# Second mixture: VectorE's two-SBUF-input operations moved in its order away from GpSimd's differences

## The chip, the cores and the metric

The kernel runs on 1 core of one Trainium2 chip. The metric is device time in microseconds (us), and the time of a version is the median of its runs. A profiled execution has a time of its own and a span, from its first instruction to its last.

## What is computed

Three layers in a row, in float32 (the weights come as float64), for 4 x 3072 tokens of 256 features:

```
scores = z @ z.T / 3072;  x = u * (max(scores, 0)**2 @ v)          # attention
k = max(mix(x, mu_k) @ w_k, 0);  x = sigmoid(mix(x, mu_r) @ w_r) * (k*k @ w_v)   # first mixture
out = ((x @ w_a) * (x @ w_b)) @ w_out                               # second mixture
```

The change lies in the second mixture alone: 12288 tokens, 256 features in and out, 1536 columns in `w_a` and `w_b`.

## The kernel before

**Precision.** Each float32 operand of a matmul is a pair: a high part rounded to float32r and a low part, the rest. ScalarE makes the high part with a copy (`high`, L1012), VectorE makes the low part with a subtraction of two SBUF tensors (`low`, L1015; L905 for the operands of the next pair). A product is three matmuls of 128x128 by 128x512: high by high, high by low, low by high.

**Units.** `mixture2` handles 12 pairs of blocks of 512 tokens (index j). For each pair it goes through 12 groups of columns (index f), so there are 144 units u = 12 j + f, and two more to drain. Each unit forms 2x2 block products with seven multiplications instead of eight (`PRODUCTS`, 1 to 7; L964), in three PSUM banks: `px`, `pw` and `py`, out of four. The order of a unit's matmuls is written out in `unit(u)`: product 1 of u; products 3 and 4 of the unit before (V = u - 1); products 2, 5 and 6 of u; two fillers; product 7 of u; the remaining fillers. A filler is one multiplication (three matmuls, L993 to L995) by `w_out` of work two units back or of the pair before. Units with f = 2 to 7 have three fillers, 30 matmuls in all; those with f = 8 to 11, and f = 0 and 1 of the next pair, have four, 33 matmuls.

**Around the matmuls.** Every engine works through its instructions in the order of the code, so the place of a line in `unit` is its place in its engine's queue. For V, VectorE adds product 3 (L1058, reads the bank `py`, which product 5 of u then takes), multiplies product 4 (L1073) and multiplies both (L1077, two SBUF inputs). If V is in the second half (f of V at least 6), L1087 forms both differences with the unit six earlier (`t32`), ScalarE rounds, and `low` gives `bl`; otherwise ScalarE rounds one block and `low` gives the low part of `b11`. L1141 adds product 7 of u to product 5 and frees `px` for product 4 in the next unit. GpSimd then forms one more difference from two SBUF tensors: L1149 for V in the second half, L1151 for V in the first.

**rest32.** For VV = u - 2 in the second half, `rest32` forms the low part `l32` of `t32` (128x1024, two SBUF inputs), used by the third and fourth filler of the same unit. It is called at f = 8 to 11 and f = 0 and 1 of the next pair, 6 units in 12. The high part `h32` is made by ScalarE a unit earlier.

**Hooks.** `run(slot)` calls what was hung on a unit's slots 0 to 10: loads of weights (`s_load` L935, `s4_load` L939, `o_load` L944 and L948, all on SP's queue, which takes them in order, each waiting for a free buffer of a pool of 25; weights asked for in unit k are first used in unit k + 2); the end of the pair before (`turn`, a transpose on VectorE, and `leave`, the stores); and the operands of the next pair, which need four differences t1 to t4 on GpSimd (`value`, L891) with high and low parts of these and of b11, b21 and b22.

Of the kernel before, what the change touches and what calls it, by code (L numbers as in the profile page):

```python
# [9 lines left out]
F32R = mybir.dt.float32r  # L10
# [17 lines left out]
def tile_kernel(  # L28
# [61 lines left out]
    def g_tile(shape, dtype, name):  # L90
        return gp.tile(shape, dtype, tag="g", name=name)
# [498 lines left out]
    def late_tile(shape, dtype, name):  # L590
        return late["p"].tile(shape, dtype, tag="m", name=name)

    def w_tile(dtype, name):
        return late["w"].tile([P, 2, QB], dtype, tag="w", name=name)
# [328 lines left out]
    def mixture2():  # L923
        NU = NP * NF2
        HALF = NF2 // 2
        back, forms, acc, ot, on, hooks = {}, {}, {}, {}, {}, {}
        sw, ow = {}, {}

        def hook(u, slot, *fns):
            hooks.setdefault((u, slot), []).extend(fns)  # L930
# [19 lines left out]
        def product(u, bank, n, first, end):  # L950
            j, f = divmod(u, NF2)
            a, b = PRODUCTS[n]
            t = t_t[j][b]
            r = u // 2
            if a == "s4":
                w = sw["D", r]
                c = f % TPB * P
                wh, wl = w[:, 0, c : c + P], w[:, 1, c : c + P]
            else:
                pair, k = PAIRS[a]  # L960
                c = f % 2 * P
                wh, wl = (sw[pair, r][:, k, h * (QB // 2) + c : h * (QB // 2) + c + P] for h in range(2))
            for m, (w, y) in enumerate(((wh, 0), (wh, 1), (wl, 0))):
                nc.tensor.matmul(  # L964
                    bank, w, t[:, y, :], start=first and m == 0, stop=end and m == 2, skip_group_check=True
                )
# [44 lines left out]
        def high(dst, src):  # L1011
            nc.scalar.activation(dst, src, AF.Copy)  # L1012

        def low(dst, src, hi):
            nc.vector.tensor_tensor(dst, src, hi.bitcast(F32), op=ALU.subtract)  # L1015

        def rest32(w, j, q):
            h, l, t = w["h32"], late_tile([P, 2, QB], F32R, "l32"), w["t32"]
            low(l, t, h)
            forms[j, q] |= {n: (h[:, k, :], l[:, k, :]) for k, n in enumerate(("t2", "t3"))}  # L1020

        def unit(u):
            j, f = divmod(u, NF2)
            go = u < NU
            v, vv = u - 1, u - 2
            V = back[v] if 0 <= v < NU else None
            VV = back[vv] if 0 <= vv < NU else None
            vj, vf = divmod(v, NF2)
            wj, wf = divmod(vv, NF2)
            vq, wq = vf % HALF, wf % HALF  # L1030
            v2, w2 = vf >= HALF, wf >= HALF
            todo = fillers(u) if go else []

            def run(slot):
                for fn in hooks.pop((u, slot), ()):
                    fn()
# [9 lines left out]
            if go:  # L1046
                x, w = U["x"], U["w"] = ps_tile("px"), ps_tile("pw")
                product(u, x, 1, True, False)
                nc.scalar.activation(w, x, AF.Copy)  # L1049
            if VV and w2 and vv < NU - 1:  # L1050
                rest32(VV, wj, wq)
            run(0)

            if V:
                cc = V["cc"]
# [6 lines left out]
            if VV and not w2:  # L1062
                t1 = w_tile(F32R, "th")
# [17 lines left out]
            if VV and w2:  # L1081
                h = g_tile([P, 2, QB], F32R, "t4")
                high(h[:, 0, :], VV["cc"][:, 0, :])
                VV["h4"] = h
            if V and v2:
                t = V["t32"] = back[v - HALF]["cc"]
                nc.vector.tensor_tensor(  # L1087
                    t, cc[:, 1, :].unsqueeze(1).to_broadcast([P, 2, QB]), t, op=ALU.subtract
                )
# [23 lines left out]
            if VV and w2:  # L1113
                h = VV["h4"]
                low(h[:, 1, :], VV["cc"][:, 0, :], h[:, 0, :])
                forms[wj, wq]["t4"] = (h[:, 0, :], h[:, 1, :])
            if V:
                if not go:
                    rest32(V, vj, vq)
                if v2:  # L1120
                    h, l = w_tile(F32R, "bh"), w_tile(F32R, "bl")
                    high(h, cc)
                    low(l, cc, h)
                    forms[vj, vq] |= {n: (h[:, k, :], l[:, k, :]) for k, n in enumerate(("b21", "b22"))}
                else:
                    h = w_tile(F32R, "b11")
                    high(h[:, 0, :], cc[:, 0, :])
                    low(h[:, 1, :], cc[:, 0, :], h[:, 0, :])
                    forms[vj, vq] = {"b11": (h[:, 0, :], h[:, 1, :])}
            run(5)  # L1130

            fill()
# [2 lines left out]
            fill()  # L1135
            run(7)

            if go:
                product(u, x, 7, False, False)
                cu = U["cc"] = g_tile([P, 2, QB], F32, "cc")  # L1140
                nc.vector.tensor_tensor(cu[:, 1, :], x, m5, op=ALU.add)  # L1141
# [28 lines left out]
        def turn(j, n, d):  # L1170
            if (j, n) not in on:
                on[j, n] = stp.tile([P, QB // SQ, ND, SQ], F32, tag="st", name="on")
            o = on[j, n]
            nc.vector.transpose(o[:, :, d, :], ot[j, n][:, d, :].rearrange("p (b i) -> p b i", i=SQ))

        def leave(j, n, queues=None):
            queues = queues or [nc.sync] * 4
            o = on.pop((j, n))
            r = out[(2 * j + n) * QB : (2 * j + n + 1) * QB, :]
            for a, dst in enumerate(r.rearrange("(b i) (a h j) -> a i b (h j)", i=SQ, h=ND, j=SQ)):  # L1180
                queues[a].dma_start(dst, o[a * SQ : (a + 1) * SQ].rearrange("i b h j -> i b (h j)"))
# [4 lines left out]
        def middle(j):  # L1186
            acs = acc[j]
            acs["B"] = accp.tile([P, QB], F32, tag="acc", name="oacc")
            nc.scalar.activation(acs["B"], acs["A"], AF.Copy)
# [17 lines left out]
        def c12_out(j):  # L1207
            scaled(ot[j, 1][:, 0, :], acc[j].pop("D"))
# [17 lines left out]
        for j in range(NP):  # L1226
            u = j * NF2
            hook(u + 7, 8, lambda j=j: middle(j))
            hook(u + 7, 9, lambda j=j: middle2(j))
            if j < NP - 1:  # L1230
                e = u + NF2
                hook(e + 1, 8, lambda j=j: c11_out(j))
                hook(e + 1, 10, lambda j=j: a_copy(j))
                hook(e + 2, 0, lambda j=j: add_to(j, "D"))
                hook(e + 2, 1, lambda j=j: add_to(j, "G"))
                hook(e + 2, 2, lambda j=j: c12_out(j))
                hook(e + 2, 3, lambda j=j: c22_sum(j))
                hook(e + 2, 8, lambda j=j: c22_out(j))
                hook(e + 3, 6, lambda j=j: turn(j, 1, 0))
                hook(e + 3, 9, lambda j=j: turn(j, 1, 1), lambda j=j: leave(j, 1))  # L1240
                hook(e + 4, 9, lambda j=j: turn(j, 0, 0))
                hook(e + 7, 10, lambda j=j: c21_out(j))
                hook(e + 8, 8, lambda j=j: turn(j, 0, 1), lambda j=j: leave(j, 0))
            if j:
                value, hi, lo = prep(j)
                todo = [
                    (1, 8, hi["b11"]), (2, 3, value["t1"]), (2, 9, lo["b11"]),
                    (3, 3, value["t2"]), (3, 7, hi["t1"]), (3, 8, lo["t1"]), (3, 8, hi["b21"]),
                    (4, 3, value["t4"]), (4, 4, lo["b21"]), (4, 7, hi["t2"]), (4, 8, lo["t2"]),
                    (5, 3, value["t3"]), (5, 6, hi["t4"]), (5, 7, lo["t4"]), (5, 8, hi["t3"]),  # L1250
                    (6, 4, lo["t3"]), (6, 8, hi["b22"]), (7, 4, lo["b22"]),
                ]
                for f, slot, fn in todo:
                    hook(u - NF2 + f, slot, fn)
                hook(u - NF2, 3, lambda j=j: y_load(j))
            for r in range(HALF):
                R = j * HALF + r
                k = 2 * R - 2
                if R > 1:
                    hook(k, 0, lambda R=R: s_load(R, "A"), lambda R=R: s_load(R, "B"))  # L1260
                    hook(k, 1, lambda R=R: s_load(R, "C"))
                    if R % 2 == 0:
                        hook(k - 1 if R > 2 else k, 3, lambda R=R: s4_load(R))
                loads = {
                    0: [(j - 1, 2, 2), (j - 1, 3, 2)],
                    1: [(j - 1, 4, 0), (j, 1, 0)],
                    2: [(j, 1, 1)],
                    3: [(j - 1, 4, 1), (j, 1, 2)],
                    4: [(j, 2, 0), (j, 3, 0)],
                    5: [(j, 2, 1), (j, 3, 1)],  # L1270
                }[r]
                for l in loads:
                    if l[0] >= 0:
                        hook(max(k, 0), 7, lambda l=l: o_load(*l))
        j = NP - 1
# [100 lines left out]
    with tc.manual_schedule():  # L1376
# [9 lines left out]
        turn, high, low = z_prep(0, 0)  # L1386
# [55 lines left out]
```

## Time and profile before

| what | value |
|---|---|
| median of 3 runs | 2589.59 us (2589.27 to 2591.72) |
| profiled execution, its own time | 2590.21 us |
| its span | 2588.4 us |
| TensorE busy with matmuls (PE) | 2554.8 us, 11112 matmuls |
| VectorE (DVE) busy | 2124.8 us |
| ScalarE (ACT) busy | 1847.3 us |
| GpSimd (POOL) busy | 326.2 us |
| second mixture without its drain, in the span | 1515.3 to 2566.7 us |

Busy time is the union of an engine's instructions. Matmuls overlap in the records, so TensorE counts as busy even where it gets on more slowly than it could; the number of matmuls in a stretch tells its pace. PEld is the loading of a matmul's 128x128 weights, which goes on beside the matmul before it.

### The profile page before, as it was taken

To read this page: it belongs to the slowest core of one execution; us is meant where nothing else is said; L and a number is where in the kernel's file an instruction comes from. 1 tells how busy PE (TensorE), PEld (TensorE's weight loads), DVE (VectorE), ACT (ScalarE), POOL (GpSimd) and SP (SyncE) were. 2 spreads that over 40 slices of the span, in tenths; PEclk is the share of its full clock that TensorE was granted. 3 is DMA by queue.
4 is the path that set the end of the run, shared out by engine and by line. 5 is a ranking of instruction groups with operands and counts; after the bars stand their busy time and mean duration, and the time that the engine had idled before them with its cause. 6 is when DMAs were issued, how large, how long until landed. Compare 5 with 4: busy or idle time off the path is not lost.

```text
span 2588.4 us, 32030 instructions
## 1 busy us (share of the span) xinstructions
PE 2554.8 (99%) x11112; PEld 2082.7 (80%) x11112; DVE 2124.8 (82%) x2785; ACT 1847.3 (71%) x2538; POOL 326.2 (13%) x320
## 2 busy tenths in 40 slices
PE   8999999999999999999999999999999999999998
PEld 6887888788788887888888877788788778877886
DVE  9887888788778778778787769888888988898888
ACT  7866977787588658878888766666666666666655
POOL 0010100010001100000000012222122222222211
PEclk9999999999999999999999999999999999999999
DMA  8788779767967793121121255665766575657563
GB/s 211 216 232 199 247 204 248 203 220 230 216 184 215 219 256 103 49 96 51 58 90 49 78 191 187 205 218 175 252 207 208 180 255 193 222 196 239 188 200 121
DMA packets 326017, 473.18 MB, mean 183 GB/s; under 512 B 192544, under 2 KB 205856, under 8 KB 318176
## 3 DMA queue, kind: packets, MB, share of 16 engines
q1 hardware_dynamic: 304832, 372.31, 49.6%
q0 software_dynamic: 18384, 98.31, 9.9%
q8 instruction: 87, 1.43, 0.2%
q10 hardware_dynamic: 2640, 0.52, 0.1%
q14 instruction: 74, 0.61, 0.1%
HBM read 347.60 MB, written 123.47 MB: 182 GB/s over the span
## 4 chain that ended last, share of the span: by engine, by line
PE 91%; DVE 3%; ACT 2%; DMA 2%; issue 1%; SPq 0%; DVEq 0%; ACTq 0%
PE px L964 14%; PE acc L101 9%; PE acc L102 9%; PE acc L100 9%; PE py L964 8%; PE px L682 5%; PE oacc L995 4%; PE oacc L993 4%; PE oacc L994 4%; PE pw L964 3%; PE vacc L100 3%; PE vacc L101 3%; PE vacc L102 3%; PE sc L440 3%; PE sc L441 3%; PE py L682 2%
## 5 line engine op out<-in xcount | busy, mean ns | idle before, releaser
L101 PE MATMUL acc<-lo,vhi 128*128 128x512 f32 x1152 | 451.3, 392 | 3.9 <-DVE lo L502 3.9
L100 PE MATMUL acc<-hi,vhi 128*128 128x512 f32 x1152 | 450.3, 391 | 3.1 <-ACT hi L499 1.9
L102 PE MATMUL acc<-hi,vlo 128*128 128x512 f32 x1152 | 450.1, 391 | 0.0
L964 PE MATMUL px<-t,sw 128*128 128x512 f32 x1296 | 365.1, 390 | 0.1
L964 PEld LDWEIGHTS px<-t,sw 128*128 128x128 f32 x1296 | 243.2, 188 | 52.6 <-DVE cc L1141 0.7
L101 PEld LDWEIGHTS acc<-lo,vhi 128*128 128x128 f32 x1152 | 217.1, 188 | 51.9 <-DVE lo L502 7.0
L100 PEld LDWEIGHTS acc<-hi,vhi 128*128 128x128 f32 x1152 | 217.2, 189 | 50.1 <-ACT hi L499 3.3
L453 ACT ACTIVATE p<-sc 128x1024 f32<-128x1024 f32 x167 | 170.6, 1021 | 116.9 <-PE sc L441 115.5
L102 PEld LDWEIGHTS acc<-hi,vlo 128*128 128x128 f32 x1152 | 217.3, 189 | 44.7
L1049 ACT ACTIVATE pw<-px 128x512 f32<-128x512 f32 x144 | 84.1, 584 | 201.7 <-PE px L964 201.7
L460 DVE STREAM_TRANSPOSE pt<-p 128x512 f32<-128x512 f32 x240 | 156.2, 689 | 74.6 <-ACT p L454 71.5
L1151 POOL TENSOR_TENSOR cc<-cc 128x512 f32<-128x512 f32 x72 | 96.8, 1344 | 881.4 <-DVE b L1015 674.0
L502 DVE TENSOR_TENSOR lo<-p,hi 128x1024 fp32r<-128x1024 f32 x167 | 199.7, 1196 | 4.9
L454 ACT ACTIVATE p<-p 128x1024 f32<-128x1024 f32 x167 | 177.2, 1061 | 5.3
L502 DVE TENSOR_TENSOR lo<-pm,hi 128x1024 fp32r<-128x1024 f32 x120 | 146.0, 1217 | 34.0 <-ACT hi L499 34.0
L1099 ACT ACTIVATE c<-pw 128x512 f32<-128x512 f32 x144 | 86.3, 599 | 117.7 <-PE pw L964 98.8
L101 PE MATMUL vacc<-kl,w 128*128 128x512 f32 x384 | 149.7, 390 | 0.6 <-DVE kl L753 0.6
L1149 POOL TENSOR_TENSOR cc<-cc 128x512 f32<-128x512 f32 x71 | 91.6, 1290 | 459.4 <-DVE bl L1015 285.2
L102 PE MATMUL vacc<-kh,w 128*128 128x512 f32 x384 | 149.5, 389 | 0.0
L100 PE MATMUL vacc<-kh,w 128*128 128x512 f32 x384 | 149.5, 389 | 0.0
L440 PE MATMUL sc<-q,kt 128*128 128x512 f32 x336 | 133.1, 396 | 6.6 <-DVE q L373 6.5
L1015 DVE TENSOR_TENSOR l<-cc,h 128x1024 fp32r<-128x1024 f32 x72 | 138.6, 1926 | 0.5 <-ACT h L1012 0.5
(194 smaller groups left out, 6018.8 us busy)
## 6 DMA issues: line engine op xcount, KB each, us to landing
sw<-kept SPq DMA_DIRECT2D x252, 512.0 KB, 5.9
pkept<-pt POOLq DMA_DIRECT2D x60, 1024.0 KB, 6.0
pm<-pkept SPq DMA_DIRECT2D x240, 256.0 KB, 6.4
ow<-kept SPq DMA_DIRECT2D x120, 512.0 KB, 7.1
kept<-w POOLq DMA_DIRECT2D x42, 512.0 KB, 5.6
vst<-in_v SPq DMA_DIRECT2D x24, 512.0 KB, 7.6
ust<-in_u SPq DMA_DIRECT2D x192, 64.0 KB, 4.6
xkept<-x POOLq DMA_DIRECT2D x24, 512.0 KB, 4.1
```

The lines of the kernel that those rows point to most:

```text
L100: nc.tensor.matmul(ps, wh, ah, start=first, stop=False)
L101: nc.tensor.matmul(ps, wh, al, start=False, stop=False)
L102: nc.tensor.matmul(ps, wl, ah, start=False, stop=last)
L440: nc.tensor.matmul(sc[:, t, :], k, q_t[b, qb][:, 0, :], start=True, stop=False)
L453: nc.scalar.activation(p, sc, AF.Relu, scale=1.0 / S)
L454: nc.scalar.activation(p, p, AF.Square)
L460: nc.vector.transpose(pt[:, :, 2 * pr + t, :], p[:, t, :].rearrange("p (c i) -> p c i", i=SQ))
L502: nc.vector.tensor_tensor(l, p, h.bitcast(F32), op=ALU.subtract)
L682: nc.tensor.matmul(bank, w[x][:, c], t[:, y, :], start=first and m == 0, stop=end and m == 2, skip_group_check=True)
L964: nc.tensor.matmul(bank, w, t[:, y, :], start=first and m == 0, stop=end and m == 2, skip_group_check=True)
L993: nc.tensor.matmul(acs[bank], wh, hi, start=first, stop=False, skip_group_check=True)
L1015: nc.vector.tensor_tensor(dst, src, hi.bitcast(F32), op=ALU.subtract)
```

## The change

`rest32` moves from the start of a unit, ahead of L1058, to behind L1077. The low part of `b11` moves from its place behind the high part to just ahead of product 7, behind slot 7. In the hooks, the transposes move from slots 6 and 9 to slots 4 and 8, the four differences of the next pair move to slot 9, right behind GpSimd's own difference of the unit, and all low parts of the next pair to slot 4; the high parts are at slot 8. Several of these come up to a unit earlier. No instruction is added or removed.

```diff
-            if VV and w2 and vv < NU - 1:
-                rest32(VV, wj, wq)
             run(0)
...
                 VV["h4"] = h
+                if vv < NU - 1:
+                    rest32(VV, wj, wq)
             if V and v2:
                 t = V["t32"] = back[v - HALF]["cc"]
...
-                    h = w_tile(F32R, "b11")
-                    high(h[:, 0, :], cc[:, 0, :])
-                    low(h[:, 1, :], cc[:, 0, :], h[:, 0, :])
-                    forms[vj, vq] = {"b11": (h[:, 0, :], h[:, 1, :])}
+                    b11 = w_tile(F32R, "b11")
+                    high(b11[:, 0, :], cc[:, 0, :])
             run(5)
...
             run(7)
 
+            if V and not v2:
+                low(b11[:, 1, :], cc[:, 0, :], b11[:, 0, :])
+                forms[vj, vq] = {"b11": (b11[:, 0, :], b11[:, 1, :])}
             if go:
                 product(u, x, 7, False, False)
...
-                hook(e + 3, 6, lambda j=j: turn(j, 1, 0))
-                hook(e + 3, 9, lambda j=j: turn(j, 1, 1), lambda j=j: leave(j, 1))
-                hook(e + 4, 9, lambda j=j: turn(j, 0, 0))
+                hook(e + 3, 4, lambda j=j: turn(j, 1, 0))
+                hook(e + 3, 8, lambda j=j: turn(j, 1, 1), lambda j=j: leave(j, 1))
+                hook(e + 4, 8, lambda j=j: turn(j, 0, 0))
...
-                    (1, 8, hi["b11"]), (2, 3, value["t1"]), (2, 9, lo["b11"]),
-                    (3, 3, value["t2"]), (3, 7, hi["t1"]), (3, 8, lo["t1"]), (3, 8, hi["b21"]),
-                    (4, 3, value["t4"]), (4, 4, lo["b21"]), (4, 7, hi["t2"]), (4, 8, lo["t2"]),
-                    (5, 3, value["t3"]), (5, 6, hi["t4"]), (5, 7, lo["t4"]), (5, 8, hi["t3"]),
-                    (6, 4, lo["t3"]), (6, 8, hi["b22"]), (7, 4, lo["b22"]),
+                    (1, 8, hi["b11"]), (1, 9, value["t1"]), (2, 4, lo["b11"]),
+                    (2, 8, hi["t1"]), (2, 9, value["t2"]), (3, 4, lo["t1"]), (3, 8, hi["b21"]),
+                    (3, 8, hi["t2"]), (3, 9, value["t4"]), (4, 4, lo["b21"]), (4, 4, lo["t2"]), (4, 8, hi["t4"]),
+                    (4, 9, value["t3"]), (5, 4, lo["t4"]), (5, 8, hi["t3"]),
+                    (5, 8, hi["b22"]), (6, 4, lo["t3"]), (6, 4, lo["b22"]),
```

## Rows read from the trace of the kernel before

**Rows 1.** The page, part 1: busy time of each engine, share of the span, instructions.

```profile
PE 2554.8 (99%) x11112; PEld 2082.7 (80%) x11112; DVE 2124.8 (82%) x2785; ACT 1847.3 (71%) x2538; POOL 326.2 (13%) x320
```

**Rows 2.** Busy time by stretch: f = 2 to 7, then f = 8 to 1.

```profile
core 0: us, PE busy (x) PEld busy (x) DVE busy (x) ACT busy (x) POOL busy (x), PEclk, DMA share, GB/s
2142.66:2183.50 40.84, 40.84 (x181) 33.78 (x180) 32.99 (x50) 26.95 (x47) 12.00 (x10) 1.00 0.59 198
2183.50:2230.72 47.22, 46.68 (x199) 36.63 (x198) 43.51 (x50) 29.64 (x46) 9.39 (x8) 1.00 0.67 220
```

**Rows 3.** Waits of weight loads, second mixture: us in total, times, longest us.

```profile
PEld py L964 <- DVE u L1058: 35.7, 75, 1.2
...
PEld px L964 <- DVE cc L1141: 0.7, 2, 0.6
```

**Rows 4.** Groups by line and shape, second mixture: busy us, mean ns | idle before, releaser.

```profile
L1015 DVE TENSOR_TENSOR l<-cc,h 128x1024 fp32r<-128x1024 f32 x70 | 135.4, 1934 | 0.0
L964 PE MATMUL py<-t,sw 128*128 128x512 f32 x432 | 130.5, 410 | 7.5 <-DVE u L1058 6.3 <-ACT c L1099 0.7
L964 PE MATMUL pw<-b,sw 128*128 128x512 f32 x432 | 122.8, 393 | 0.5 <-ACT pw L1049 0.5
...
L964 PE MATMUL py<-b,sw 128*128 128x512 f32 x429 | 120.5, 389 | 0.0
...
L1015 DVE TENSOR_TENSOR bl<-cc,bh 128x1024 fp32r<-128x1024 f32 x71 | 87.0, 1225 | 19.9 <-ACT bh L1012 19.4
```

**Rows 5.** Timeline of a unit with f = 11: start us, us, instruction.

```profile
1941.52 0.68 DVE L1141 TENSOR_TENSOR cc<-px,m 128x512 f32<-128x512 f32 x1
...
1941.82 1.29 POOL L1149 TENSOR_TENSOR cc<-cc 128x512 f32<-128x512 f32 x1 [6.50 <-DVE bl L1015]
1941.95 0.84 PE L964 MATMUL px<-b,sw 128*128 128x512 f32 x3
1942.12 2.08 DVE L1015 TENSOR_TENSOR l<-cc,h 128x1024 fp32r<-128x1024 f32 x1
...
1944.12 0.68 DVE L1058 TENSOR_TENSOR u<-py,u 128x512 f32<-128x512 f32 x1
...
1944.85 0.96 PE L964 MATMUL py<-t,sw 128*128 128x512 f32 x3
...
1945.32 0.68 DVE L1077 TENSOR_TENSOR cc<-u,cc 128x512 f32<-128x512 f32 x1
...
1945.65 0.85 PE L964 MATMUL px<-t,sw 128*128 128x512 f32 x3
...
1946.03 1.23 DVE L1087 TENSOR_TENSOR cc<-cc 128x1024 f32<-128x1024 f32 x1
...
1947.08 1.05 ACT L1012 ACTIVATE bh<-cc 128x1024 fp32r<-128x1024 f32 x1
1947.17 0.69 DVE L1015 TENSOR_TENSOR t<-cc,t 128x512 fp32r<-128x512 f32 x1
...
1948.17 1.22 DVE L1015 TENSOR_TENSOR bl<-cc,bh 128x1024 fp32r<-128x1024 f32 x1 [0.31 <-ACT bh L1012]
...
1949.61 1.29 POOL L1149 TENSOR_TENSOR cc<-cc 128x512 f32<-128x512 f32 x1 [6.50 <-issue]
```

**Rows 6.** Timeline of the end of f = 6 and of f = 7, without rest32.

```profile
1909.94 0.69 DVE L1015 TENSOR_TENSOR b<-cc,b 128x512 fp32r<-128x512 f32 x1 [0.69 <-ACT b L1012]
...
1911.31 0.84 PE L964 MATMUL px<-b,sw 128*128 128x512 f32 x3
...
1912.87 0.69 DVE L1058 TENSOR_TENSOR u<-py,u 128x512 f32<-128x512 f32 x1 [1.35 <-PE py L964]
...
1914.03 0.84 PE L964 MATMUL py<-t,sw 128*128 128x512 f32 x3
...
1914.16 0.68 DVE L1077 TENSOR_TENSOR cc<-u,cc 128x512 f32<-128x512 f32 x1
```

**Rows 7.** Second mixture: SP's wait for rest32's buffers; landing of the loads of sw.

```profile
SPq L935 <- DVE l L1015: 118.6, 23, 7.0
...
DMA to landing us min/median/max: 3.3/5.9/11.1
```

## Prediction

> **What bounds the kernel now.** I read the page first: the reader is to see TensorE at 99% of the span and VectorE at 82%, so time can only come from places where TensorE, although it counts as busy, gets on too slowly [rows 1]. The change touches only the second mixture, so I cut one pair of blocks of that stage into its two halves and asked for the busy time of each. The six units f = 2 to 7 take 40.84 us for 180 matmuls, 0.2269 us each, with VectorE busy for 33.0 us. The six units f = 8 to 11 and f = 0, 1 of the next pair take 47.22 us for 198 matmuls, 0.2385 us each, with VectorE busy for 43.5 us [rows 2]. At the pace of the first half, 198 matmuls take 198 x 0.2269 = 44.92 us, so each second half loses 47.22 - 44.92 = 2.30 us. I call its units full units: they are the ones with four fillers, and the ones that call rest32.
>
> The waits say where. In all of the second mixture TensorE's weight loads wait 75 times on `u L1058`, 35.7 us in total, and on nothing else in VectorE but 0.7 us for `cc L1141` [rows 3]. By lines, the matmuls of product 5 (`py<-t,sw`) last 410 ns in the mean, where the same shape lasts 389 ns in product 3, and have 7.5 us of idle time ahead of them [rows 4].
>
> The timeline of one full unit shows why [rows 5]. Count from the first matmul of product 1, at 1941.95. L1141 runs, GpSimd's difference L1149 starts at 1941.82, and the low part `l<-cc,h` of rest32 starts at 1942.12. It takes 2.08 us; the low part of the same shape `bl<-cc,bh` takes 1.23 us in the same unit and 1225 ns in the mean of 71, against 1934 ns for the 70 of rest32 [rows 4, 5]. L1058 can only follow, at 1944.12. It frees the bank that product 5 writes, and product 5 starts at 1944.85, 2.90 us after product 1. In a unit without rest32, L1058 starts 1.56 us after product 1 and product 5 starts 2.72 us after it [rows 6].
>
> VectorE's own order in this unit has no room: its instructions follow each other from L1141 at 1941.52 to `bl` at 1948.17 and then L1141 again [rows 5], 7.8 us in all against 33 x 0.2269 = 7.49 us of matmuls. So the full units run at VectorE's pace, and 0.85 us of it is rest32 beside GpSimd.
>
> On that overlap the page "SBUF — State Buffer" of the Trainium skill, section "Who interferes with whom", says that a VectorE instruction with two SBUF inputs and a GpSimd instruction that reads SBUF exclude each other for the whole instruction, whichever starts first. The trace agrees here: GpSimd ends at 1943.11, and 1.09 us later, at 1944.20, rest32's low part is done, about what such an instruction takes if it begins at GpSimd's end. If instead any VectorE work beside GpSimd lost 0.85 us, the sum below would stay as it is, because VectorE has 0.90 us idle where GpSimd will run.
>
> **The change part by part.** *rest32 goes behind L1077.* It issues one VectorE instruction and no DMA. I lay out a full unit from rows, product 1 at 0. L1058 starts at 1.56 and L1077 at 2.85 [rows 6]. An instruction of 512 columns holds VectorE for 0.60 us (L1058 to L1077 is two of them in 1.20 us), one of 1024 columns alone for 1.14 us (L1087 at 1946.03 to `t` at 1947.17) [rows 5]. So rest32 runs from 3.45, L1087 from 4.59, the low part of t4 from 5.73, `bl` from 6.33. For `bl` ScalarE's `bh` must be done: it starts 1.43 us after product 6 does and `bl` 1.09 us after that [rows 5]; product 6 starts after 15 matmuls, at 3.40, so `bl` could start at 5.92, and it is VectorE's order that sets 6.33. L1141 follows at 7.47 and ends at 8.15. The next unit begins at 7.49.
>
> What is late next, and by how much it is not. Product 5 needs L1058's end at 2.24 and starts at 2.72: 0.48 us to spare. The third filler needs rest32's result at its third matmul, the thirtieth of the unit: 29 x 0.2269 = 6.58, and it is there at 3.45 + 1.23 = 4.68. Product 4 of the next unit adds to the bank that L1141 reads: it starts at 7.49 + 1.36 = 8.85, and L1141 is done at 8.15, 0.70 us to spare, the tightest place. GpSimd's difference starts 1.44 us after `bl` [rows 5], at 7.77, and ends at 9.06, beside L1141 (one input in PSUM; it took 0.68 us beside GpSimd at 1941.52 [rows 5]) and an idle VectorE (8.15 to 9.05, when the next L1058 is due). The next L1077, with two SBUF inputs, comes at 7.49 + 2.85 = 10.34, 1.28 us after. So nothing waits for VectorE any more and the unit takes 7.49 us.
>
> Sum: 70 of these low parts lie ahead of the drain, 70 / 6 = 11.7 halves x 2.30 = 26.8 us. What stays is product 2's wait on ScalarE's L1049, which the change doesn't touch: the 432 matmuls of `pw` last 393 ns instead of 389, 1.7 us [rows 4]. Gain 26.8 - 1.7 = 25.1 us. Bounds: TensorE's own rows alone give 432 x 21 ns + 7.5 us = 16.6 us for product 5 [rows 4]; more than 26.8 us would need time outside the full units.
>
> *The SP queue that rest32 is moved past.* rest32 is the last reader of a `cc` buffer, and loads of `sw` wait for it: SP waited 23 times on it, 118.6 us [rows 7]. Its end goes from 2.25 us after product 1 to 4.68, so such a load is issued up to 2.4 us later, with those behind it. Loads asked for in unit k are first used in unit k + 2, about 15 us on, and land 5.9 us after issue in the median, 11.1 us at most [rows 7]. No row of the waits has TensorE waiting for a load. I cost it at nothing; without that cover it is the rival on the other side.
>
> *Low part of b11 behind the fillers, the transposes and low parts of the next pair at slots 4 and 8, differences at slot 9.* All of it lies in units with f = 1 to 6, where VectorE is busy for 33.0 of 40.8 us and TensorE keeps its pace [rows 2]. Two differences in a row hold GpSimd for about 2 x 1.29 us [rows 5] after the low part of b11 `b<-cc,b`, which ends 0.7 us before the next unit [rows 6]; with about 0.2 us for GpSimd to start they end 2.0 us into it, ahead of L1077 at 2.85. Nothing gained, and nothing lost as long as L1058 ends before 2.72. Low parts freed from GpSimd there save VectorE time that nobody waits for: zero. ScalarE's high parts move with them and are no more in number. *The drain:* the same L1058, L1077, rest32 and L1087 in another order before the chain that ends the kernel; L1087 comes at about the same time. Zero, within about 1 us either way.
>
> **The rivals.** *The wait moves to product 4 (12%).* L1141 now ends a long run of VectorE. If one of the four long instructions still meets GpSimd and takes 0.85 us more, L1141 ends 0.85 - 0.70 = 0.15 us late in each full unit: 70 x 0.15 = 10.5 us come back, gain 14.6 us, 2575 us. For it: the margin is the smallest one. Against it: now product 4 waits on L1141 twice in all [rows 3], and GpSimd is released by `bl`, the last of the run.
>
> *No change (5%).* L1058 would have been held not by rest32 but by product 3, or GpSimd's difference would slide along to the new place. Then 2589 to 2591 us. Against it: L1058 starts 2.17 us after product 1, 0.61 us later than in a unit without rest32 [rows 5, 6], and just as rest32 ends.
>
> *Slower by the loads (4%).* If `sw` loads released by rest32 landed just when TensorE needs them, each of the 23 waits would pass on 2.4 us: 55 us lost against 25 gained, about 2619 us. The place is product 1 of the unit after next; it breaks even where the loads have 25.1 / 23 = 1.1 us less to spare than the 2.4 us. Against it: some 15 us of lead against a landing of 5.9 us.
>
> **How the numbers follow.** The forecast as told, 79%. The profiled execution took 2590.21 us, 0.62 us over the median of the runs, and the gain of 25.1 us comes off it: 2565.1 us in that execution, 2564.5 us as a median. The range begins at 2560, where the wait for ScalarE and a little of the other units go too, and ends at 2574, where only the 16.6 us of TensorE's own rows come back; it leaves out the rivals and a little of the forecast, 2 in 10. A kernel whose runs lie within 0.1% of each other tells 0.2%, 5 us, from no change. Faster by more than that: 0.91 (the forecast and the first rival); within it 0.05; slower 0.04.
>
> **What would show it.** In the profile after: rest32's low part at about 1.23 us and behind L1077; the 75 waits on `u L1058` gone from the full units; product 5 at 2.72 us after product 1; full halves of about 45.1 us, other halves unchanged at 40.8. Wrong, if weight loads wait on `cc L1141` or on `sw`, if GpSimd's L1149 grows or starts beside L1077, or if the halves with f = 2 to 7 get longer.

## The result, and the profile after

The changed kernel takes 2561.49 us (median of 5 runs, 2559.63 to 2564.64) against 2589.49 us before (5 runs, 2588.93 to 2591.72): 28.0 us less, ratio 0.9892, 95% interval 0.9878 to 0.9907. The forecast was 2564.5 us. The profiled execution took 2563.22 us (span 2561.5 us), against 2590.21 us: 27.0 us less. In the changed kernel some lines have other numbers: L1058 is L1056, L1073 is L1071, L1077 is L1075, L1141 is L1142 and L1149 is L1150.

The two halves of the same pair of blocks as in [rows 2], f = 2 to 7 and then f = 8 to 1:

```profile
2126.33:2167.13 40.80, 40.80 (x181) 33.81 (x180) 32.23 (x49) 26.96 (x47) 11.13 (x10) 1.00 0.64 216
2167.13:2212.19 45.06, 45.06 (x199) 37.12 (x198) 39.37 (x50) 30.18 (x46) 9.38 (x8) 1.00 0.68 223
```

The first half is as it was. The second, the one with the full units, went from 47.22 to 45.06 us: 0.2276 us for a matmul instead of 0.2385. VectorE is busy there for 39.4 us instead of 43.5 with as many instructions.

All that the weight loads of the second mixture still wait for, up to the end of the drain (answers to [rows 3]: us in total, times, longest us):

```profile
PEld pw L964 <- ACT pw L1049: 3.9, 12, 0.9
PEld oacc L995 <- DVE l L1015: 1.1, 1, 1.1
PEld py L964 <- ACT c L1099: 1.1, 1, 1.1
PEld px L964 <- DVE cc L1142: 0.9, 2, 0.6
PEld oh L995 <- DVE t L1015: 0.7, 1, 0.7
```

The 75 waits on `u L1058`, 35.7 us, are gone altogether; the 12 on ScalarE's L1049 are what they were, and no load of weights is waited for. By lines (answers to [rows 4]):

```profile
L964 PE MATMUL pw<-b,sw 128*128 128x512 f32 x432 | 122.9, 393 | 0.5 <-ACT pw L1049 0.5
L964 PE MATMUL py<-t,sw 128*128 128x512 f32 x432 | 121.6, 390 | 0.7 <-ACT c L1099 0.7
...
L1015 DVE TENSOR_TENSOR bl<-cc,bh 128x1024 fp32r<-128x1024 f32 x71 | 86.6, 1220 | 7.7 <-ACT bh L1012 7.7
...
L1015 DVE TENSOR_TENSOR l<-cc,h 128x1024 fp32r<-128x1024 f32 x70 | 85.3, 1219 | 0.0
```

rest32's low part now lasts 1219 ns, as long as `bl` of the same shape, and the matmuls of product 5 (`py<-t`) 390 ns, next to the 389 ns of product 3 in [rows 4]. The timeline of a full unit (answers to [rows 5]: start us, us, instruction):

```profile
1930.19 1.22 DVE L1015 TENSOR_TENSOR bl<-cc,bh 128x1024 fp32r<-128x1024 f32 x1
...
1931.33 0.69 DVE L1142 TENSOR_TENSOR cc<-px,m 128x512 f32<-128x512 f32 x1
1931.35 0.84 PE L964 MATMUL px<-b,sw 128*128 128x512 f32 x3
1931.56 1.29 POOL L1150 TENSOR_TENSOR cc<-cc 128x512 f32<-128x512 f32 x1 [6.19 <-DVE bl L1015]
...
1932.91 0.69 DVE L1056 TENSOR_TENSOR u<-py,u 128x512 f32<-128x512 f32 x1 [0.90 <-PE py L964]
...
1934.07 0.84 PE L964 MATMUL py<-t,sw 128*128 128x512 f32 x3
1934.20 0.68 DVE L1075 TENSOR_TENSOR cc<-u,cc 128x512 f32<-128x512 f32 x1
...
1934.80 1.22 DVE L1015 TENSOR_TENSOR l<-cc,h 128x1024 fp32r<-128x1024 f32 x1
...
1935.94 1.22 DVE L1087 TENSOR_TENSOR cc<-cc 128x1024 f32<-128x1024 f32 x1
...
1937.07 0.69 DVE L1015 TENSOR_TENSOR t<-cc,t 128x512 fp32r<-128x512 f32 x1
...
1937.67 1.22 DVE L1015 TENSOR_TENSOR bl<-cc,bh 128x1024 fp32r<-128x1024 f32 x1
1938.81 0.69 DVE L1142 TENSOR_TENSOR cc<-px,m 128x512 f32<-128x512 f32 x1
1938.83 0.84 PE L964 MATMUL px<-b,sw 128*128 128x512 f32 x3
```

GpSimd's difference (L1150) lies beside L1142, which has one input in PSUM, and beside an idle VectorE: ahead of L1056 VectorE is idle for 0.90 us, until product 3 releases it. Neither takes longer for it, L1142 0.69 us and L1150 1.29 us.

### The profile page after: what moved, and what is told of

Its sections match the earlier page's. It is cut to its first block, busy times and chain, and to the rows that moved or that the text cites. A ratio compares the mean times of both kernels' runs of the same rounds, so it can differ in the third digit from the quotient of the medians.

```text
span 2561.5 us, 31977 instructions
## 1 busy us (share of the span) xinstructions
PE 2533.0 (99%) x11112; PEld 2087.0 (81%) x11112; DVE 2066.4 (81%) x2785; ACT 1855.2 (72%) x2538; POOL 316.7 (12%) x320
## 4 chain that ended last, share of the span: by engine, by line
PE 90%; issue 3%; DMA 2%; DVE 2%; ACT 1%; SPq 0%; POOL 0%; DVEq 0%; ACTq 0%; POOLq 0%
PE px L964 15%; PE acc L101 8%; PE acc L102 8%; PE acc L100 8%; PE py L964 8%; PE px L682 5%; PE oacc L995 4%; PE oacc L993 4%; PE oacc L994 4%; PE pw L964 4%; PE vacc L101 3%; PE vacc L100 3%; PE vacc L102 3%; PE sc L441 3%; PE sc L440 3%
## 5 line engine op out<-in xcount | busy, mean ns | idle before, releaser
L1049 ACT ACTIVATE pw<-px 128x512 f32<-128x512 f32 x144 | 84.1, 584 | 199.4 <-PE px L964 199.4
L1056 DVE TENSOR_TENSOR u<-py,u 128x512 f32<-128x512 f32 x144 | 99.6, 692 | 126.9 <-PE py L964 126.9
L1150 POOL TENSOR_TENSOR cc<-cc 128x512 f32<-128x512 f32 x71 | 91.7, 1292 | 441.0 <-DVE bl L1015 218.0
```

## The experiments

Each is compared with runs of the kernel before on the same chip. **First, which part of the change does it.** Only rest32 is moved; the low part of b11 and the hooks stay:

```diff
-            if VV and w2 and vv < NU - 1:
-                rest32(VV, wj, wq)
...
                 VV["h4"] = h
+                if vv < NU - 1:
+                    rest32(VV, wj, wq)
```

> The kernel before with rest32 moved behind the product of both sums, and nothing else. Theory (the full units ran at VectorE's pace because rest32's low part lay beside GpSimd's difference ahead of L1058): nearly the whole gain, the full halves at 45.0 us instead of 47.2, 70 / 6 x 2.2 = 25.5 us, so about 2564 us; the other halves keep the waits of up to 0.3 us that they had, some 1.3 us in all. Rival (the hooks and the low part of b11 are half of it): about 2576 us.

Measured: 2562.50 us against 2589.13, ratio 0.9899 (0.9882 to 0.9915). The move of rest32 alone brings back 26.6 us, all of the gain that the times can tell. The counterpart, everything but that move:

```diff
+            if VV and w2 and vv < NU - 1:
+                rest32(VV, wj, wq)
             run(0)
...
                 VV["h4"] = h
-                if vv < NU - 1:
-                    rest32(VV, wj, wq)
```

> The changed kernel with rest32 back at the start of the unit. Theory: the full halves stay at 47.2 us and the low part of rest32 at 1.93 us; only the waits in the other halves go, about 1.3 us, so 2588 us, not to be told from before. Rival (the hooks and the low part of b11 are half of it): about 2576 us.

Measured: 2585.85 us against 2589.13, ratio 0.9992 (0.9983 to 1.0002): not told from no change. Its profile took 2585.24 us, 5.0 us less than that of before, but 3.9 us of this arose before the second mixture, whose first L1049 started at 1511.4 us instead of 1515.3; the stages before it are the same code. In the mixture the old wait is still there, as its weight loads say:

```profile
PEld py L964 <- DVE u L1058: 34.3, 69, 1.2
```

**Second, is it the order or the overlap?** The order of before, with GpSimd's difference of the second-half units left out:

```diff
-                    (SIDE if go else nc.vector).tensor_tensor(cc[:, 0, :], cc[:, 0, :], V["t32"][:, 0, :], op=ALU.subtract)
+                    if not go:
+                        nc.vector.tensor_tensor(cc[:, 0, :], cc[:, 0, :], V["t32"][:, 0, :], op=ALU.subtract)
```

> The kernel before, order and all, without GpSimd's difference L1149 (left out in the 71 units that have it on GpSimd, so one operand keeps its value from before the difference). Theory (the overlap with GpSimd is the cost): rest32's low part falls from 1.93 to about 1.23 us where it stands, VectorE's work in a full unit from 7.8 to 6.9 us, below the 7.49 us of matmuls; L1058 starts on product 3 again and the whole gain appears without any move, about 2563 us. Rival (it is the order: L1058 behind a long instruction is late whatever that takes): 2585 us or more, with the weight loads still waiting on L1058.

Measured: 2564.94 us against 2589.13, ratio 0.9908 (0.9893 to 0.9922). With rest32 where it was, its low part falls to 1211 ns and nine tenths of the waits go. Lines and waits of this run:

```profile
L1015 DVE TENSOR_TENSOR l<-cc,h 128x1024 fp32r<-128x1024 f32 x70 | 84.8, 1211 | 0.0
```

```profile
PEld py L964 <- DVE u L1058: 3.4, 17, 0.5
```

So the order by itself costs 17 short waits, and the overlap cost the rest.

**Third, how near the next bound is.** The changed kernel gets one more GpSimd instruction in each full unit, timed by the end of L1056 so that it lies beside the product of both sums:

```diff
                     nc.vector.tensor_tensor(V["u1"], V["y"], V["u1"], op=ALU.add)
+                    if go and VV and w2:
+                        SIDE.tensor_tensor(late["spare"], V["u1"], V["u1"], op=ALU.add)
```

> The changed kernel with one more GpSimd instruction in each full unit: a sum of u1 with itself into a spare buffer, which becomes ready with the end of the sum of product 3 and so lies beside the product of both sums and ahead of rest32. Theory (two SBUF inputs wait until GpSimd is done, and the tightest place after the change is product 4 behind L1141, 0.70 us): the product of both sums ends about 0.8 us later and all of VectorE's run behind it, L1141 ends at 8.97 instead of 8.15 us, product 4 starts 0.12 us late in each of 70 units: 8 us and a little more for the restart of TensorE, about 2571 us, weight loads of px waiting on L1141. Rival (only the place of L1058 ahead of the long instructions counts, GpSimd doesn't matter): 2561.5 us as after the change.

Measured: 2563.82 us against 2589.13, ratio 0.9905 (0.9890 to 0.9919). The overlap came about and the loss did not. One unit of its timeline (L1075 of the changed kernel is L1077 here):

```profile
1940.58 1.04 POOL L1058 TENSOR_TENSOR spare<-u 128x512 f32<-128x512 f32 x1 [0.49 <-DVE u L1056]
...
1941.04 1.12 DVE L1077 TENSOR_TENSOR cc<-u,cc 128x512 f32<-128x512 f32 x1
```

The sum took 1.04 us, not 1.29, and the product ended 0.54 us after it: 0.44 us longer than alone, less than the 0.70 us to spare. So it was too weak a test of that place, and I had mis-sized it. A longer one reads two blocks and has 896 columns:

```diff
+                    if go and VV and w2:
+                        n = late["spare"].shape[2]
+                        SIDE.tensor_tensor(
+                            late["spare"],
+                            V["u1"][:, :n].unsqueeze(1).to_broadcast([P, 2, n]),
+                            VV["cc"][:, 1, :n].unsqueeze(1).to_broadcast([P, 2, n]),
+                            op=ALU.add,
+                        )
```

> The changed kernel with a longer GpSimd instruction beside the product of both sums than the sum in the run before last: 896 columns from two blocks into a spare buffer, ready with the end of the sum of product 3. That run showed that 0.44 us of delay fit into the 0.70 us to spare. Theory: GpSimd lasts 1.8 to 2.3 us, the product of both sums ends 0.55 us after it, 1.4 to 1.8 us later than without; product 4 then starts late in each full unit by half of what is over 0.70 us (the delay also moves the unit that it ends in), 0.35 to 0.55 us, 70 times, so 25 to 39 us: 2587 to 2600 us, as slow as before the change or slower, with weight loads of px waiting on L1141. Rival (there is no such tight place, VectorE's order alone counts): 2562 to 2566 us.

Measured: 2606.07 us against 2589.03, ratio 1.0068 (1.0053 to 1.0083): slower than before the change, and 44.6 us over the changed kernel. One unit of its timeline (L1075 of the changed kernel is L1083 here, and L1142 is L1150), and what the weight loads of `px` waited for in this run up to 2540 us:

```profile
1963.23 0.84 PE L964 MATMUL px<-b,sw 128*128 128x512 f32 x3
...
1964.27 0.68 DVE L1150 TENSOR_TENSOR cc<-px,m 128x512 f32<-128x512 f32 x1
...
1965.00 0.97 PE L964 MATMUL px<-t,sw 128*128 128x512 f32 x3 [0.26 <-DVE cc L1150]
1965.69 2.13 POOL L1059 TENSOR_TENSOR spare<-u,cc 128x896 f32<-128x896 f32 x1
...
1966.62 1.76 DVE L1083 TENSOR_TENSOR cc<-u,cc 128x512 f32<-128x512 f32 x1
```

```profile
PEld px L964 <- DVE cc L1150: 46.6, 56, 1.3
```

The sum ends at 1967.82, the product of both sums at 1968.38, 0.56 us later: 5.15 us after product 1 instead of 3.53. That is 1.62 us, 0.92 us over what there was to spare. In this layout half of it, 0.46 us, is what each unit grows by: product 4 of the next unit starts late by that much and shifts all that follows, the next product 1 too, which takes up the other half. The trace bears this out: TensorE is idle ahead of product 4 for 25.3 us in 59 units, 0.43 us each. With the restart (the three matmuls of product 4 take 0.97 instead of 0.84 us) a unit should grow by 0.59 us. It grows by 0.61 us: from one L1049 to the one six units on, the full units of the same pair take 48.27 us instead of 44.61. In 70 units this is 43 us of the 44.6. The measured time lies 6 us above the expected range. The delay of 1.62 us is one that the expectation allowed for (1.4 to 1.8 us); what it left out is the restart, 0.13 us in each of 70 units, 9 us.

The room on VectorE can also be filled: the difference of the second-half units goes to VectorE, in the changed kernel:

```diff
-                    (SIDE if go else nc.vector).tensor_tensor(cc[:, 0, :], cc[:, 0, :], V["t32"][:, 0, :], op=ALU.subtract)
+                    nc.vector.tensor_tensor(cc[:, 0, :], cc[:, 0, :], V["t32"][:, 0, :], op=ALU.subtract)
```

> The changed kernel with the difference L1149 of the second-half units on VectorE instead of GpSimd. Theory: VectorE is idle for 0.90 us in a full unit, between L1141 and the next L1058, just where this instruction of 0.60 us falls, so the time stays at 2561.5 us within 0.2%. Rival (VectorE is the bound of the full units again as soon as anything is added): 70 x 0.6 us more at worst, up to 2600 us.

Measured: 2561.27 us against 2589.03, ratio 0.9896 (0.9881 to 0.9910), the changed kernel's time, without this instruction on GpSimd.

**Fourth, what in GpSimd's instruction is in the way.** In the order of before, the difference becomes a fill of the same block, a copy with one input (`SIDE.tensor_copy(cc[:, 0, :], V["t32"][:, 0, :])` in the place of the fill), and a fill of twice the size (`SIDE.memset(cc, 0.0)`):

```diff
-                    (SIDE if go else nc.vector).tensor_tensor(cc[:, 0, :], cc[:, 0, :], V["t32"][:, 0, :], op=ALU.subtract)
+                    if go:
+                        SIDE.memset(cc[:, 0, :], 0.0)
+                    else:
+                        nc.vector.tensor_tensor(cc[:, 0, :], cc[:, 0, :], V["t32"][:, 0, :], op=ALU.subtract)
```

> The kernel before, order and all, with GpSimd's difference L1149 replaced by filling the same block with zeros (this leaves the difference out): GpSimd writes SBUF beside rest32's low part but reads none. Theory, narrowed: what rest32 waits for is GpSimd's reading, so the low part falls to 1.23 us as in the run without any GpSimd instruction there, and the time is 2563 to 2565 us. Rival (any GpSimd instruction in SBUF holds up VectorE's two-input ones): the low part stays near 1.9 us, less by what the fill is shorter than the difference, and the time lies near 2589 us, in any case over 2575.

> The kernel before, order and all, with GpSimd's difference L1149 replaced by a copy of t32's block (this leaves the difference out): one SBUF input in place of two. Theory: a read by GpSimd holds up rest32's low part whether it has one input or two, for as long as the copy lasts; if the copy takes about half of the 1.29 us, the low part takes some 1.4 us and the full units are again at or near the pace of the matmuls, 2564 to 2572 us. Rival (only an instruction with two inputs on GpSimd is in the way): the low part at 1.23 us.

> The kernel before, order and all, with GpSimd's difference L1149 replaced by filling both blocks of the buffer with zeros (this leaves the difference out and destroys the second block): the fill of one block took 0.53 us and ended 0.12 us after rest32's low part had begun, too little to tell whether a GpSimd instruction that only writes is in the way. Two blocks take about 1.05 us and lie beside the low part for some 0.65 us. Theory (only GpSimd's reading is in the way): the low part stays at 1.21 us. Rival (any GpSimd instruction in SBUF is in the way): the low part ends 1.08 us after the fill, as it did after the copy and the difference, so it takes about 1.7 us, and waits of the weight loads on L1058 come back in all the full units.

Measured: 2561.94 us against 2589.03, ratio 0.9896 (0.9880 to 0.9913), for the fill; 2562.57 us, ratio 0.9899 (0.9885 to 0.9914), for the copy; 2561.85 us against 2587.74, ratio 0.9903 (0.9886 to 0.9919), for the longer fill. The time alone says little here, since 0.2 us more of rest32 still fits; the timelines tell them apart (L1149 is L1150 in these runs). The copy:

```profile
1943.64 0.61 POOL L1150 COPY cc<-cc 128x512 f32<-128x512 f32 x1 [6.87 <-DVE bl L1015]
1943.94 1.39 DVE L1015 TENSOR_TENSOR l<-cc,h 128x1024 fp32r<-128x1024 f32 x1
```

It ends at 1944.25, 0.31 us into rest32's low part, which ends 1.08 us later and so lasts 0.18 us longer than alone. The longer fill:

```profile
1937.57 0.96 POOL L1150 MEMSET cc<- 128x1024 f32 x1 [6.53 <-DVE bl L1015]
1937.98 1.22 DVE L1015 TENSOR_TENSOR l<-cc,h 128x1024 fp32r<-128x1024 f32 x1
1939.37 0.69 DVE L1058 TENSOR_TENSOR u<-py,u 128x512 f32<-128x512 f32 x1 [0.17 <-PE py L964]
```

It lies beside the low part for 0.55 us and the low part lasts 1.22 us. A read by GpSimd, of one input or two, holds the low part up for as long as it lasts; a fill, which only writes, does not. The short fill could not show this, its overlap was 0.12 us. The fills stand in the difference's place in GpSimd's order, so it was not the mere presence of a GpSimd instruction there that cost the time.

**Last, the drain.** rest32 stays ahead of L1058 in the first draining unit alone:

```diff
+            if VV and w2 and vv < NU - 1 and not go:
+                rest32(VV, wj, wq)
             run(0)
...
-                if vv < NU - 1:
+                if vv < NU - 1 and go:
```

> The changed kernel with rest32 left ahead of L1058 in the first of the two draining units alone, where the changed kernel has TensorE wait 1.1 us on rest32's low part. Theory: that wait goes, but the chain that ends the kernel runs through L1058, L1087 and ScalarE, which come no earlier, so the time is the same within 0.2%: 2561 us, at most 1 us less. Rival (the drain's wait lies on the path to the end): 0.9 us less, which the trace's last 30 us would show.

Measured: 2561.86 us against 2587.74, ratio 0.9902 (0.9887 to 0.9917): as the changed kernel. The wait for rest32 does not vanish, it goes to the next rest32, 1.0 us; from the last L1049 to the end it takes 28.6 us, against 28.3 in the changed kernel and 28.6 before. The low part that was put back lies beside GpSimd again and takes 2.07 us. In the changed kernel the chain of work that ended last does run through the low part that TensorE waits for (1.15 us at 2542.70); here it runs through the next one (1.24 us at 2544.64), so the expectation was wrong to leave it off the path, and yet nothing is gained by moving it. No version faster than the changed one by more than can be measured came out of these runs.

## Why the prediction was right

- *Where the time was.* Right: the full units ran at VectorE's pace because rest32's low part waited for GpSimd. Without the overlap the same order loses almost nothing (2564.9 us), with the move alone nearly all comes back (2562.5 us).
- *The unit after the change.* Laid out from rows, it came true step by step. Forecast and measured, in us after product 1: L1058 1.56 and 1.56, product 5 2.72 and 2.72, L1077 2.85 and 2.85, rest32 3.45 and 3.45, L1087 4.59 and 4.59, the low part of t4 5.73 and 5.72, `bl` 6.33 and 6.32, L1141 7.47 and 7.46. The next unit came at 7.48 instead of 7.49 us.
- *The sum.* Right in its main term: 2.16 us for the full half shown, against 2.30 less the wait on L1049; by the starts of L1049 all full units together gave 25.1 us, as forecast. The halves f = 2 to 7, costed at nothing, gave 1.5 us in all: taken from the start of L1049 at f = 2 to that at f = 8, the twelve come to 492.1 us instead of 493.6. No run shows what gave it: the move of rest32 alone brings them to 492.3 us, all but that move to 492.6. The rest of the 27.0 us are 0.2 us ahead of the mixture and 0.3 us in the drain. The median fell by 1.0 us more than the profiled execution, which lies 1.7 us over its own median.
- *The hooks and the low part of b11.* Right, nothing that the times can tell: 2585.85 us without the move of rest32, not told from before, and 2562.50 us with that move alone.
- *The wait moves to product 4.* The place is right, its price was wrong. That a delay of 0.85 us costs 0.15 us in each unit took no account of the shift of the unit itself: 0.44 us cost nothing that can be told, and 1.62 us cost 0.6 us in each unit, which made the kernel slower than before.
- *The loads.* Ruled out here: for `sw`, SP waits on rest32 11 times and 30.9 us in all (L935 once, L939 ten times) instead of 23 times and 118.6 us, and TensorE waits on no load.
- *The drain.* Right as a whole, 28.3 us instead of 28.6. But TensorE's weight loads wait there for rest32 for 1.1 us (0.6 us before), and the chain that ended last runs through that wait, which I had not seen; putting that low part earlier gained nothing.

## What to carry to other kernels

Where TensorE is busy at 99% and yet slow, compare its matmuls per us in stretches of the same kind of work, and where one is slower, look for an instruction of another engine that lasts longer there than its twins of the same shape. Two instructions that get in each other's way can be parted by order alone, with none added or removed: put the one that needs both inputs from SBUF where GpSimd is silent, and GpSimd beside instructions that read PSUM. Before moving a long instruction, write down what it is then ahead of and how much that has to spare; here it was 0.70 us, and going 0.92 us over it cost more than the move had gained.

## What the runs showed of the hardware

- A VectorE instruction with two SBUF inputs that begins beside a GpSimd instruction that reads SBUF ends a fixed time after GpSimd does. The low part of 1024 columns ended 1.06 to 1.09 us after it (71 times in the kernel before, 60 times in the run with the copy), the product of 512 columns 0.54 to 0.59 us (70 times in each run with a sum), whatever the length of GpSimd's instruction (0.61, 1.04, 1.29 and 2.13 us).
- The wait goes the other way too. Eleven times in the kernel before, GpSimd's L1151 begins 0.2 us into a low part of the next pair, and it takes 1.61 or 1.62 us instead of 1.29. In the changed kernel, with the differences and these low parts in other slots, the 72 of them take 1.29 us in the mean. One of the eleven:

```profile
1903.75 0.68 DVE L905 TENSOR_TENSOR t<-tv,t 128x512 fp32r<-128x512 f32 x1
1903.97 1.62 POOL L1151 TENSOR_TENSOR cc<-cc 128x512 f32<-128x512 f32 x1 [3.58 <-PE oacc L995]
```

- Beside GpSimd's longer fill (0.96 us) the low part took 1.21 to 1.22 us, as without GpSimd. That a GpSimd instruction that only writes SBUF does not contend with such a VectorE instruction is what the page "SBUF — State Buffer" of the Trainium skill states in the section "Who interferes with whom", and this run agrees.
- On GpSimd a sum of a block with itself took 1.04 us, the difference of two blocks of the same size 1.29 us, a copy 0.61 us and a fill 0.53 us.
- The stages ahead of the second mixture, the same code in all 12 profiles, took from 1511.2 to 1515.8 us. Differences of a few us between profiled executions have to be looked for in the stretch that was changed.
